# Seven part products for a third group of four expert tiles in a Fourier and expert layer on one core

## The chip, the core and the metric

The kernel runs on one core of one Trainium2 chip. Its engines work side by side: PE (TensorE) multiplies 128 x 128 weight tiles with columns that stream past them, and PEld is PE's loading of those weights; DVE (VectorE) and ACT (ScalarE) do element-wise work and can read the accumulators (PSUM banks); POOL (GpSimd) does element-wise work on SBUF only; SP (SyncE) issues nearly all DMAs from one queue, in order. Each engine runs its own instruction list in order, so an instruction that waits holds up everything behind it on that engine.

The metric is the device time of one execution in microseconds (us); less is better. The profile is one further execution, recorded instruction by instruction.

## The reference

The layer takes 2048 tokens of width 512, normalizes them, and adds three things: the input, a two-dimensional Fourier transform of the normalized input (given as matrices; real part), and an expert layer that picks 2 of 4096 experts per token and head.

```python
xn = _layernorm(x)
return x + _A_ref(xn, ...) + _B_ref(xn, ...)

# A: y = Cr @ (xn Wr^T) - Ci @ (xn Wi^T)
# B, with 32 heads, dk = 128, 64 x 64 = 4096 experts:
q = einsum("nd,dhc->nhc", xf, w_q)
s1 = einsum("nhd,ed->nhe", q[..., :dk], k1)
s2 = einsum("nhd,ed->nhe", q[..., dk:], k2)
# two best of s1 and of s2, their 4 sums, the 2 best of those -> top_e, top_s
g = softmax(top_s)
act = gelu(einsum("nd,nhkd->nhk", xf, u[top_e]))
out = einsum("nhk,nhk,nhkd->nd", g, act, v[top_e])
```

## The kernel before

**Precision.** Float32 operands are split into a float16 high part and a float16 low part, and a product is three matmuls (high-high, high-low, low-high) into a float32 bank.

**Stages.** (1) Up to about 77 us: layer norm and the Fourier part. (2) The score stage, to 420 us: for each of 8 chunks of 4 heads (`j`) and 16 token tiles of 128 (`i`), PE computes the scores (`s_mm`, line 252), ACT moves them out of the bank (line 951), DVE finds the largest ones (lines 955, 959), and `routing` on POOL, DVE and ACT turns the indices of a chunk into experts and weights. In the same 128 steps, at step numbers set by hand in the list `todo`, ACT and POOL prepare everything that the later stages read: they scale and split `w_q` (`m_prep`, lines 162 to 167), the expert inputs `u` and outputs `v` (`fill_uv`, lines 780 to 782), and store in DRAM the sums of `u` blocks (`sum_u`) and of token blocks (`sum_x`). (3) The expert stage, to the end: rather than gather, the kernel multiplies every token with all 4096 experts (`z` phases, 16 groups of 256 experts), makes a one-hot weight matrix from the routing (`g_mm`, PE line 1252, fed by DVE lines 1242 to 1250), multiplies it with the activations (`w_part`) and multiplies the outcome with all of `v` (`v` phases, line 1297).

**A pair phase.** Six of the `z` phases handle two token tiles at once (tiles 2 and 3, 4 and 5, to 12 and 13); between two of them stand two `v` phases. A group of 256 experts is multiplied in one of two ways:

- *plain tile*, `u_part` (line 1095, "c" in the order string): 24 matmuls of 256 columns, one bank, then two GELUs on ACT (line 1102) that empty the bank;
- *part products*, `slot` (line 1164): four groups together (a "quad") are seen as a 2 x 2 by 2 x 2 block product, which takes 7 block products in place of 8 when some of them are made from sums of blocks. Each part product is 24 matmuls of 128 columns. The part products 1, 6, 7, 4 add up in one bank (X), 5 and 3 in another (Z), 2 has a third (Y), and between them ACT copies intermediate values out (lines 1198, 1203, 1205, 1211), DVE adds (1200, 1208, 1212) and ACT applies the GELU (1191). PE may add to X again only when ACT has copied the value before.

Before the change groups 8 to 15 form two quads, groups 0 to 7 are plain. The order of a pair phase is a string, quads a and b:

```python
SEQ = "1a 5a 2a c 6a c 3a c 7a c 1b 5b 4a 2b c 6b c 3b 7b c c 4b".split()
```

Four banks (`banks`) go round in the order in which they were given back, so PE can also wait for the bank that it takes next. Part products 5, 6, 7 and 3 read a sum of `u` blocks (512 KB), which is loaded from DRAM into a ring of three buffers. `ring_plan` decides beforehand, from nominal durations, which buffer each load takes and after which part product it is issued; `ring_load` issues it on SP.

**Checks along the way.** The kernel checks that the given matrices are the Fourier matrices and that nothing overflows; a slower general path follows if not. For that, "units" load pieces of the inputs during the expert stage: `compare` loads a tile `cx` (lines 1326, 1327), DVE subtracts what it should be (1328 to 1353), ACT sums what is left (1373); `fit` loads `w_q` (1424) for ACT to sum. A pair phase has three `compare` units and one `fit`.

The order of the instructions on each engine is set by a scheduler that keeps the dependencies of the program and moves instructions within them.

Of the kernel before, what the change touches and what calls it, by code (L numbers as in the profile page):

```python
# [20 lines left out]
D = 512  # L21
# [7 lines left out]
XS = 512.0  # L29
V1 = 5  # L30
V2 = 9
QUADS = (8, 10, 12, 14), (9, 11, 13, 15)
PAIRS = tuple(range(2, 14, 2))


# [1 line left out]
def tile_fnet_peer(ctx, tc, x, ca, cb, c5, wt, wf, wr, wq, kt, ut, vn, out):  # L37
# [117 lines left out]
    def m_prep(j, t, pool, at):  # L155

        raw = MS[j, t].rearrange("p h k -> p (h k)")
        MS[j, t, "h"] = pool.tile([P, 2, D], F16, tag="wh", name=f"wh{j}_{t}", bufs=4)
        h = MS[j, t, "h"].rearrange("p h k -> p (h k)")
        l = raw.bitcast(F16)[:, 0:2 * D]  # L160
        MS[j, t, "l"] = l.rearrange("p (h k) -> p h k", h=2)
        nc.scalar.activation(h, raw, AF.Copy, scale=at)
        if t > (1 if j == 2 else 0):
            nc.scalar.activation(raw, raw, AF.Copy, scale=at)
        else:
            nc.gpsimd.tensor_scalar(raw, raw, sw, None, op0=ALU.mult)
        nc.gpsimd.tensor_tensor(l, raw, h, op=ALU.subtract)
# [553 lines left out]
    def part_b(safe, stS, stP, stQ, stE, xt, u_sb, cmp_p, w4):  # L721
# [65 lines left out]
        def scratch(g):  # L787
            return v_sb[g].rearrange("p l c d -> p (l c d)").bitcast(F32)
# [11 lines left out]
        def sum_u(g, part, at=None):  # L800

            qd, t = next((n, q.index(g)) for n, q in enumerate(QUADS) if g in q)
            s4 = scratch(8 - t % 2)
            if part == 0:
                raw = SRAW.pop(g)
                a = [raw[:, c, k * 256:k * 256 + 256] for c in range(2) for k in range(2)]
                r = [s4[:, k * 256:k * 256 + 256] for k in range(4)]
                nc.gpsimd.tensor_tensor(r[0], a[2], a[3], op=ALU.add)
# [4 lines left out]
            split4(part - 1, s4, v_sb[6].rearrange("p l c d -> p (l c d)")[:, t % 2 * 2 * D:t % 2 * 2 * D + 2 * D],  # L813
                   lambda i: s_d[qd].rearrange("o p (t l f) -> t l p o f", t=4, l=2)[t, i], at)

        def sum_x(b, part, at=None):

            n = (0, 2, 4, 5, 7, 5)[PAIRS.index(b)]
            f, t4 = scratch(n), scratch(n + 1)
            if part == 0:  # L820
                v = xq[b // 2]
                nc.gpsimd.tensor_copy(f[:, 0:1], behind(one, at))
                nc.gpsimd.tensor_tensor(f.rearrange("p (q f) -> p q f", q=2),  # L823
                                        v[:, :, 0].rearrange("p q k n -> p q (k n)"),
                                        v[:, :, 1].rearrange("p q k n -> p q (k n)"), op=ALU.add)
                b11, b21, b12, b22 = [f[:, k * 256:k * 256 + 256] for k in range(4)]
# [149 lines left out]
        else:  # L976
# [12 lines left out]
        fills = [divmod(n, 16) for n in (0, 1, 2, 8, 3, 10, 16, 4, 12, 14, 17, 5, 9, 11, 18, 6, 13, 15, 19, 7, 20,  # L989
                                         21, 22, 23, 24)]  # L990
        slots = [29, 31, 36, 43, 45] + [16 * j + i for j in range(3, 7) for i in (4, 6, 11, 13)]
        slots += [119 + 2 * n for n in range(len(fills) - len(slots))]
        assert fills[slots.index(119)] == (1, V1)
        for (which, g), n in zip(fills, slots):
            todo[n].append(lambda at, w=which, g=g: fill_uv(w, g, at))
            todo[n - (3 if n < 119 else 1)].append(lambda at, w=which, g=g: fill_load(w, g))
            if which == 0 and not safe and any(g in q for q in QUADS):
                todo[n + 5].append(lambda at, g=g: (sum_u(g, 1, at), sum_u(g, 2)))
        if not safe:
            for n, b in zip((19, 22, 25, 107, 111, 114), PAIRS):  # L1000
                todo[n].append(lambda at, b=b: sum_x(b, 0, at))
                todo[n + (4 if n == 114 else 5)].append(lambda at, b=b: (sum_x(b, 1, at), sum_x(b, 2)))
# [101 lines left out]
        if not safe:  # L1104
            sx = stE.enter_context(tc.tile_pool(name="sx", bufs=1, side="left"))
            x4 = sx.tile([P, 2, 4, 2, P], F16, name="x4")
            PLAIN = [g for g in range(16) if not any(g in q for q in QUADS)]
            SEQ = "1a 5a 2a c 6a c 3a c 7a c 1b 5b 4a 2b c 6b c 3b 7b c c 4b".split()
            OPS = {"1": (0, None, None, 0), "2": (1, None, None, 1), "5": (None, 0, 0, None), "6": (None, 1, 1, None),
                   "3": (None, 3, None, 3), "7": (None, 2, 2, None), "4": (3, None, 3, None)}  # L1110

        USES = []
        if not safe:
            clock = 0
            for n in range(len(PAIRS)):
                for o in SEQ:
                    ns = 2616 if o == "c" else 1344
                    if o != "c" and OPS[o[0]][1] is not None:
                        USES.append((clock, clock + ns, ("ab".index(o[1]) + n) % 2, OPS[o[0]][1]))
                    clock += ns  # L1120
                clock += 50000
        RING = {}
# [48 lines left out]
        def z_pair(b, n, after):  # L1171

            cgs = iter(PLAIN)
            st = {}
            total, done, cg = sum(2616 if o == "c" else 1344 for o in SEQ), 0, 0
            for o in SEQ:
                if o == "c":
                    u_part(b, next(cgs))
                    done += 2616
                else:  # L1180
                    op, qd = o[0], ("ab".index(o[1]) + n) % 2
                    quad = QUADS[qd]

                    def dst(a, c):
                        return ACT[b[c]][:, 2 * quad[0] + a:2 * quad[3] + 2:2 * (quad[1] - quad[0]), :]

                    def v(p):
                        return p.rearrange("p (t n) -> p t n", t=4)

                    def gelu(d, src=None):  # L1190
                        nc.scalar.activation(d, d if src is None else src, AF.Gelu_apprx_tanh, scale=zsc)  # L1191

                    if op in "125":
                        st[o[1], "X" if op == "1" else "Y" if op == "2" else "Z"] = take(f"z{op}_{b[0]}_{qd}")
                    (X, Xt), (Y, Yt), (Z, Zt) = [st.get((o[1], k), (None, None)) for k in "XYZ"]
                    slot(op, quad, Z if op in "53" else Y if op == "2" else X, qd)
                    if op == "1":
                        nc.scalar.activation(dst(0, 0), v(X), AF.Copy)
                    elif op == "2":
                        nc.vector.tensor_tensor(dst(0, 0), v(Y), dst(0, 0), op=ALU.add)  # L1200
                        banks.append(Yt)
                    elif op == "5":
                        nc.scalar.activation(dst(1, 0), v(Z), AF.Copy)
# [565 lines left out]
```

## Time and profile before

| What | Value |
|---|---|
| Median of 3 runs | 1145.59 us (1145.26 to 1149.68) |
| The profiled execution's own time | 1145.57 us |
| Its span, first to last instruction | 1143.8 us |
| Busy in the span: PE, DVE, ACT, POOL | 98%, 83%, 56%, 27% |
| DMA, mean over the span | 173 GB/s |
| Score stage | about 77 to 420 us |
| Six pair phases | 490.6 to 531.9, 577.4 to 621.4, 666.8 to 710.8, 756.2 to 798.8, 844.3 to 888.4, 933.8 to 977.4 us |

A row of a timeline or of a group reads: engine, line, operation, out<-in, shapes, number of instructions, duration, and the idle time of the engine just before with the instruction that ended it ("<-"). In a timeline a merged row's duration runs to the end of its last matmul, which overlaps the next one's start; the distance from one start to the next is what it costs. PEclk is the share of the full TensorE clock that was granted.

### The profile page before, as it was taken

The numbers are of one execution on the slowest core, as the hardware profiler recorded it, in microseconds if no ns is written. First come the engines' busy times: TensorE is split into PE (matmuls) and PEld (weight loads), VectorE is DVE, ScalarE is ACT, GpSimd is POOL, SyncE is SP. The second block draws the span as 40 slices with busy tenths as digits, with TensorE's granted clock in tenths as the row PEclk, the third lists the DMA queues.
The fourth block names the chain that finished last, engine by engine and source line by source line (L and its number), as shares of the span: only waits on it lengthen the run. The fifth ranks groups of instructions, "written<-read, shape, count | busy, mean of one in ns | idle before, by whom it ended". The sixth has DMA issues, their size and how long they took to land.

```text
span 1143.8 us, 27323 instructions
## 1 busy us (share of the span) xinstructions
PE 1123.1 (98%) x10748; PEld 726.1 (63%) x10748; DVE 949.7 (83%) x2855; ACT 642.1 (56%) x1086; POOL 312.3 (27%) x342
## 2 busy tenths in 40 slices
PE   9999999999999999999999999999999999999997
PEld 6455454544544469687487488479478569567763
DVE  7899979989889899956985895895996886889782
ACT  6557598788787374454444445435435534545542
POOL 1415896887888730000000000000010010000000
PEclk8999999999999999999999999999999999999999
DMA  9884455435333216453752762763663654565743
GB/s 283 278 208 162 164 167 188 140 110 194 114 134 105 75 51 207 157 210 123 259 180 101 243 222 92 229 213 119 222 206 131 219 198 145 186 235 174 237 148 105
DMA packets 114856, 198.36 MB, mean 173 GB/s; under 512 B 34068, under 2 KB 57499, under 8 KB 114718
## 3 DMA queue, kind: packets, MB, share of 16 engines
q1 hardware_dynamic: 114416, 196.45, 51.5%
q8 instruction: 86, 1.41, 0.5%
q14 instruction: 52, 0.43, 0.1%
q10 hardware_dynamic: 302, 0.08, 0.1%
HBM read 165.75 MB, written 24.97 MB: 167 GB/s over the span
## 4 chain that ended last, share of the span: by engine, by line
PE 50%; DVE 7%; DMA 5%; POOL 2%; ACT 2%; issue 1%; SPq 0%; ACTq 0%; POOLq 0%; DVEq 0%
PE v L1297 24%; PE z L1095 14%; PE z L1164 7%; DMA cx<-in_cb_dram 4%; PE g L1252 4%; PE s L252 2%; DVE L L1242 1%; DVE w L1260 1%; DVE cx L1347 1%; DVE act L1268 1%; ACT cx L1373 1%; POOL v L823 1%; DMA fit<-in_wq_dram 1%; DVE R L1247 0%; DVE R L1250 0%
## 5 line engine op out<-in xcount | busy, mean ns | idle before, releaser
L252 PE MATMUL s<-m,xq 128*128 128x512 f16 x1344 | 297.4, 379 | 2.5 <-ACT ss L951 2.5
L1297 PE MATMUL v<-v,act 128*128 128x512 f16 x1056 | 233.3, 379 | 0.0
L252 PEld LDWEIGHTS <-xq 128*128 128x128 f16 x1344 | 129.7, 98 | 153.5 <-issue 3.8
L1095 PE MATMUL z<-xb,u 128*128 128x128 f16 (+1 forms) x2688 | 219.9, 242 | 5.0 <-ACT act L1191 4.7
L1095 PEld LDWEIGHTS <-u 128*128 128x128 f16 x2688 | 196.7, 98 | 18.2 <-issue 5.6
L1310 POOL TENSOR_TENSOR y<-y,xr 128x512 f32<-128x512 f32 x15 | 24.6, 1643 | 638.8 <-DMA y<-y_d 380.5
L1242 DVE TENSOR_TENSOR L<-io_lam,cmp 128x2048 f16<-128x2048 f16 x128 | 158.4, 1237 | 41.3 <-PE g L1252 41.3
L1297 PEld LDWEIGHTS <-act 128*128 128x128 f16 x1056 | 101.2, 98 | 117.6 <-issue 0.2
L955 DVE MAX8 vals<-ss 128x8 f32<-128x64 f32 x896 | 133.4, 216 | 3.0 <-ACT ss L951 3.0
L951 ACT ACTIVATE ss<-s,wsc 128x512 f32<-128x512 f32 x120 | 81.7, 684 | 44.1 <-PE s L252 35.5
L1297 PE MATMUL v<-v,w 128*128 128x512 f16 x480 | 106.2, 379 | 0.0
L1373 ACT ACTIVATE cx<-cx 128x896 f32<-128x896 f32 x64 | 60.4, 943 | 63.5 <-DVE cx L1353 49.0
L959 DVE FIND_INDEX8 idx<-vals,ss 128x8 uint16<-128x256 f32 x224 | 93.8, 419 | 0.0
L1267 ACT ACTIVATE act<-w 128x1024 f16<-128x1024 f32 x36 | 48.4, 1360 | 69.2 <-DVE w L1260 69.0
L1297 PEld LDWEIGHTS <-w 128*128 128x128 f16 x480 | 45.9, 98 | 53.4
L1102 ACT ACTIVATE act<-z,scl 128x256 f32<-128x256 f32 (+1 forms) x88 | 44.1, 525 | 49.5 <-PE z L1095 49.5
L1252 PEld LDWEIGHTS <-L 128*128 128x128 f16 x2048 | 60.2, 96 | 12.0 <-issue 1.5
L1260 DVE SCALAR_TENSOR_TENSOR w<-act,scl,g 128x1024 f32<-128x1024 f32 x44 | 55.7, 1276 | 13.4 <-ACT act L1191 13.4
L1347 DVE TENSOR_TENSOR cx<-cx 128x512 f32<-128x512 f32 (+2 forms) x84 | 48.4, 610 | 18.6 <-DMA cx<-in_cb_dram 18.5
L1164 PEld LDWEIGHTS <-s 128*128 128x128 f16 x1080 | 62.7, 98 | 0.5
L1252 PE MATMUL g<-R,L 128*128 128x32 f16 x2048 | 62.0, 176 | 1.0 <-DVE R L1250 0.9
L1268 DVE TENSOR_TENSOR act<-w,act 128x1024 f16<-128x1024 f32 x44 | 59.2, 1348 | 2.3 <-ACT act L1267 2.3
(363 smaller groups left out, 1729.2 us busy)
## 6 DMA issues: line engine op xcount, KB each, us to landing
v<-v_d SPq DMA_DIRECT2D x67, 512.0 KB, 4.6
cx<-in_cb_dram SPq DMA_DIRECT2D x64, 448.0 KB, 5.4
s<-s_d SPq DMA_DIRECT2D x35, 512.0 KB, 4.5
w<-in_wq_dram SPq DMA_DIRECT2D x28, 512.0 KB, 6.1
fit<-in_wq_dram SPq DMA_DIRECT2D x28, 512.0 KB, 4.3
uv<-in_vn_dram SPq DMA_DIRECT2D x16, 512.0 KB, 4.0
uv<-in_ut_dram SPq DMA_DIRECT2D x16, 512.0 KB, 4.0
c<-in_ca_dram SPq DMA_DIRECT2D x8, 512.0 KB, 7.5
```

What stands on the lines that cost most here:

```text
L252: nc.tensor.matmul(ps, xt[i][:, l, kd, :], m[:, r, kd, :], start=(n == 0), stop=(n == 3 * KD - 1))
L951: nc.scalar.activation(s, ps, AF.Copy, scale=inv)
L955: nc.vector.max(vals[:, i, w, :, h], s[:, g, :])
L959: nc.vector.max_index(idx[:, i, w].rearrange("p k h -> p (k h)"), vals[:, i, w, 0:2].rearrange("p k h -> p (k h)"), s[:, w * HC:g + 1, :]. ...
L1095: nc.tensor.matmul(ps if n == 1 else ps.rearrange("p (b n) -> p b n", b=2), ug[:, l, c % 2, kd, :], xb2[:, k0, r, kd, :] if n == 1 else xb ...
L1164: nc.tensor.matmul(bank[:, t * P:(t + 1) * P], lt, rt, start=(t == k == 0 and op in "125"), stop=(t == 3 and k == 5), skip_group_check=op ...
L1242: nc.vector.tensor_tensor(L.rearrange("p t (l two) -> p t l two", two=2), io_lam.rearrange("p (l two) -> p l two", two=2).unsqueeze(1).to_ ...
L1252: nc.tensor.matmul(p[:, hf, t * NC:(t + 1) * NC], L[:, t, :], R[:, t, :], start=True, stop=True)
L1260: nc.vector.scalar_tensor_tensor(w, act[:, :, ts], fw, p.rearrange("p h (n c) -> p c (h n)", c=NC), op0=ALU.mult, op1=ALU.mult)
L1268: nc.vector.tensor_tensor(w16[..., 1], w, w16[..., 0], op=ALU.subtract)
L1297: nc.tensor.matmul(pv, w16[:, c, :, l], v_sb[g][:, r, cc, :], start=(n + cc == 0 and k == 0), stop=(n == 15 and cc == 1 and k == 2))
L1373: later.append(lambda: nc.scalar.activation(tf[:, P:], tf[:, P:], AF.Abs, accum_out=chk[:, n:n + 1]))
```

## The change

Groups 4 to 7 become a third quad, so that only groups 0 to 3 stay plain in the pair phases; the two single-tile phases at each end keep 16 plain groups. A pair phase then has 21 part products and 4 plain tiles in place of 14 and 8, in a new order with single plain tiles between part products; in every other pair phase the quads' order is reversed (`turn_q`). The ring loads 10 sums in the second to sixth pair phase, 6 before.

In the score stage groups 4 to 7 get their sums (`sum_u`: four additions or subtractions on POOL, a copy on ACT, a subtraction on POOL, two stores of 256 KB each); ACT in place of POOL scales the first quarter of `w_q` for `j` = 3 to 7; the order of the fills and three of the steps of `sum_x` change, and with them its scratch tiles.

```diff
-QUADS = (8, 10, 12, 14), (9, 11, 13, 15)
+QUADS = (8, 10, 12, 14), (9, 11, 13, 15), (4, 5, 6, 7)
...
         nc.scalar.activation(h, raw, AF.Copy, scale=at)
-        if t > (1 if j == 2 else 0):
+        if t > 1 or j > 2:
             nc.scalar.activation(raw, raw, AF.Copy, scale=at)
         else:
             nc.gpsimd.tensor_scalar(raw, raw, sw, None, op0=ALU.mult)
...
-            s4 = scratch(8 - t % 2)
+            par = [f for w, f in fills if w == 0 and any(f in q for q in QUADS)].index(g) % 2
+            s4 = scratch(8 - par)
...
-            n = (0, 2, 4, 5, 7, 5)[PAIRS.index(b)]
+            n = (0, 2, 4, 4, 7, 5)[PAIRS.index(b)]
...
-        slots += [119 + 2 * n for n in range(len(fills) - len(slots))]
+        slots = slots[:-1] + [113] + [119 + 2 * n for n in range(4)]
...
-            for n, b in zip((19, 22, 25, 107, 111, 114), PAIRS):
+            for n, b in zip((19, 22, 25, 106, 109, 118), PAIRS):
...
-            SEQ = "1a 5a 2a c 6a c 3a c 7a c 1b 5b 4a 2b c 6b c 3b 7b c c 4b".split()
+            SEQ = "1a 5a 2a 6a c 3a 1b 7a 2b 5b 4a 6b c 3b 1c 7b 2c 5c 4b 6c c 3c 7c c 4c".split()
+
+            def turn_q(k, n):
+                return ("abc" if n % 2 else "cba").index(k)
...
-                    op, qd = o[0], ("ab".index(o[1]) + n) % 2
+                    op, qd = o[0], turn_q(o[1], n)
```

What this does to the engines' lists shows at three places. In them `cx9` to `cx11` are the tiles of three `compare` units, `z1_4_q`, `z2_4_q` and `z5_4_q` the banks X, Y and Z of quad `q` for tiles 4 and 5, `z4_n` the bank of the n-th plain tile, and `sq_k_n` a ring buffer with sum k of quad q, loaded after the n-th use of the ring. Line numbers in the changed kernel are up to 4 higher.

ACT in the second pair phase (tiles 4 and 5), before:

```order
L1373 ACTIVATE cx10_8897,sums_87<-cx10_8897 128x896
L1102 ACTIVATE act4_8248<-z4_3_8537,scl_93 128x256
L1102 ACTIVATE w4_126<-z4_3_8537,scl_93 128x256
L1373 ACTIVATE cx11_8984,sums_87<-cx11_8984 128x896
L1198 ACTIVATE act4_8248<-z1_4_0_8568 128x4x128
L1203 ACTIVATE act4_8248<-z5_4_0_8594 128x4x128
L1191 ACTIVATE act4_8248<-z1_4_1_8249,scl_93 128x4x128
```

ACT at the same place, now:

```order
L1377 ACTIVATE cx10_9070,sums_87<-cx10_9070 128x896
L1195 ACTIVATE w4_126<-w4_126,scl_93 128x4x128
L1202 ACTIVATE act4_8366<-z1_4_2_8793 128x4x128
L1377 ACTIVATE cx11_9184,sums_87<-cx11_9184 128x896
L1215 ACTIVATE w4_126<-z1_4_1_8572 128x4x128
L1195 ACTIVATE w4_126<-w4_126,scl_93 128x4x128
L1195 ACTIVATE act4_8366<-act4_8366,scl_93 128x4x128
L1207 ACTIVATE act4_8366<-z5_4_2_8923 128x4x128
L1195 ACTIVATE act4_8366<-z1_4_1_8572,scl_93 128x4x128
```

Behind the sum over `cx11` there stood two copies of the second quad and the GELU that empties bank X of the first; now the first instruction behind it is the copy of part product 7 of the second quad, which its part product 4 waits for.

SP in the same phase, before:

```order
L1424 DMA fit7_8649<-in_wq_dram 128x1024
L1326 DMA cx9_8744<-in_ca_dram 128x128
L1327 DMA cx9_8744<-in_cb_dram 128x896
L1326 DMA cx10_8897<-in_ca_dram 128x128
L1147 DMA s0_0_10_8478<-s_d_61 128x2048
L1327 DMA cx10_8897<-in_cb_dram 128x896
L1326 DMA cx11_8984<-in_ca_dram 128x128
L1327 DMA cx11_8984<-in_cb_dram 128x896
L1147 DMA s0_1_11_8532<-s_d_61 128x2048
```

SP at the same place, now:

```order
L1428 DMA fit7_8820<-in_wq_dram 128x1024
L1151 DMA s1_1_14_8569<-s_d_61 128x2048
L1330 DMA cx9_8917<-in_ca_dram 128x128
L1331 DMA cx9_8917<-in_cb_dram 128x896
L1151 DMA s1_3_15_8622<-s_d_61 128x2048
L1330 DMA cx10_9070<-in_ca_dram 128x128
L1151 DMA s1_2_16_8678<-s_d_61 128x2048
L1331 DMA cx10_9070<-in_cb_dram 128x896
L1330 DMA cx11_9184<-in_ca_dram 128x128
L1151 DMA s2_0_17_8731<-s_d_61 128x2048
L1331 DMA cx11_9184<-in_cb_dram 128x896
```

One ring load stood between the loads of the three `compare` tiles; now a ring load stands ahead of each of them, and each of those waits for PE to end a part product.

POOL early in the last chunk of the score stage (`g6` is the routing weight of chunk 6, `v6`, `v8` scratch tiles), before:

```order
L795 TENSOR_TENSOR v6_921<-v6_921,v5_920 128x1024
L924 CAST z_826<-lc6_0_5210 128x16x2x4 x2
L924 CAST z_826<-di6_0_5202 128x16x2x4 x2
L822 COPY v5_920<-ss7_2_5185 128x1
L823 TENSOR_TENSOR v5_920<-xq6_109 128x1024
L828 TENSOR_TENSOR v6_921<-v5_920 128x256
L830 TENSOR_TENSOR v6_921<-v5_920 128x256
L829 TENSOR_TENSOR v6_921<-v5_920,v6_921 128x256
L831 TENSOR_TENSOR v6_921<-v5_920,v6_921 128x256
L895 TENSOR_TENSOR g6_0_5274<-c106_0_5163,g6_0_5274 128x16x4
L795 TENSOR_TENSOR v8_923<-v8_923,v7_922 128x1024
```

POOL at the same place, now:

```order
L782 TENSOR_TENSOR v4_919<-uv1_4_5108,v4_919 128x1024
L925 CAST z_826<-lc6_0_5246 128x16x2x4 x2
L896 TENSOR_TENSOR g6_0_5308<-c106_0_5195,g6_0_5308 128x16x4
L795 TENSOR_TENSOR v8_923<-v8_923,v7_922 128x1024
L925 CAST z_826<-di6_0_5238 128x16x2x4 x2
L823 COPY v5_920<-ss7_6_5364 128x1
L824 TENSOR_TENSOR v5_920<-xq6_109 128x1024
```

The sums of the last token pair (five instructions from `xq6` on) stood ahead of the routing weight; now they stand behind it, and a fill's subtraction stands ahead.

More of the change, by code (lines that the diff above doesn't have):

```diff
@@ L812, in sum_u @@
                 return
-            split4(part - 1, s4, v_sb[6].rearrange("p l c d -> p (l c d)")[:, t % 2 * 2 * D:t % 2 * 2 * D + 2 * D],
+            split4(part - 1, s4, v_sb[6].rearrange("p l c d -> p (l c d)")[:, par * 2 * D:par * 2 * D + 2 * D],
                    lambda i: s_d[qd].rearrange("o p (t l f) -> t l p o f", t=4, l=2)[t, i], at)
         def sum_x(b, part, at=None):
-            n = (0, 2, 4, 5, 7, 5)[PAIRS.index(b)]
+            n = (0, 2, 4, 4, 7, 5)[PAIRS.index(b)]
             f, t4 = scratch(n), scratch(n + 1)
@@ L988, in part_b @@
                         lambda at, j=j, t=t: m_prep(j, t, wqp, behind(sw, at)))
-        fills = [divmod(n, 16) for n in (0, 1, 2, 8, 3, 10, 16, 4, 12, 14, 17, 5, 9, 11, 18, 6, 13, 15, 19, 7, 20,
-                                         21, 22, 23, 24)]
+        fills = [divmod(n, 16) for n in (0, 1, 2, 8, 3, 10, 4, 16, 12, 14, 5, 17, 9, 11, 6, 18, 13, 15, 7, 19, 20,
+                                         23, 24, 21, 22)]
         slots = [29, 31, 36, 43, 45] + [16 * j + i for j in range(3, 7) for i in (4, 6, 11, 13)]
-        slots += [119 + 2 * n for n in range(len(fills) - len(slots))]
-        assert fills[slots.index(119)] == (1, V1)
+        slots = slots[:-1] + [113] + [119 + 2 * n for n in range(4)]
         for (which, g), n in zip(fills, slots):
@@ L999, in part_b @@
         if not safe:
-            for n, b in zip((19, 22, 25, 107, 111, 114), PAIRS):
+            for n, b in zip((19, 22, 25, 106, 109, 118), PAIRS):
                 todo[n].append(lambda at, b=b: sum_x(b, 0, at))
-                todo[n + (4 if n == 114 else 5)].append(lambda at, b=b: (sum_x(b, 1, at), sum_x(b, 2)))
+                todo[n + (4 if n == 118 else 5)].append(lambda at, b=b: (sum_x(b, 1, at), sum_x(b, 2)))
         for g, n in zip(range(V2, 16), (25, 38, 41, 57, 73, 89, 105)):
@@ L1118, in part_b @@
                     if o != "c" and OPS[o[0]][1] is not None:
-                        USES.append((clock, clock + ns, ("ab".index(o[1]) + n) % 2, OPS[o[0]][1]))
+                        USES.append((clock, clock + ns, turn_q(o[1], n), OPS[o[0]][1]))
                     clock += ns
```

## Prediction

> **What bounds the kernel now.** I began with the busy times of the page.
>
> ```profile
> PE 1123.1 (98%) x10748; PEld 726.1 (63%) x10748; DVE 949.7 (83%) x2855; ACT 642.1 (56%) x1086; POOL 312.3 (27%) x342
> ```
>
> PE is busy for 1123.1 of 1143.8 us, so what the change does to PE's own work counts in full, and what it does elsewhere counts only where PE comes to wait. An average over stages can hide such waits; next I looked at the table of windows. Its columns are the window, its length, busy time (and instructions) of PE, PEld, DVE, ACT and POOL, the granted clock, the DMA share and GB/s. The first six rows are the pair phases, called P0 to P5 here; then come a burst inside P2 and 45 us of the score stage.
>
> ```profile
> 490.60:531.90 41.30, 41.30 (x593) 39.12 (x592) 21.16 (x49) 19.52 (x39) 1.52 (x1) 1.00 0.35 125
> 577.40:621.40 44.00, 42.55 (x631) 40.09 (x628) 29.44 (x46) 20.20 (x40) 1.48 (x1) 1.00 0.42 143
> 666.80:710.80 44.00, 42.49 (x631) 40.06 (x628) 29.58 (x47) 20.26 (x40) 2.48 (x1) 1.00 0.42 143
> 756.20:798.80 42.60, 42.28 (x631) 39.98 (x628) 29.69 (x48) 20.54 (x40) 1.74 (x1) 1.00 0.42 147
> 844.30:888.40 44.10, 42.35 (x633) 40.06 (x630) 33.08 (x62) 20.30 (x40) 1.75 (x1) 1.00 0.41 142
> 933.80:977.40 43.60, 42.51 (x632) 40.09 (x629) 29.72 (x49) 20.39 (x40) 2.35 (x1) 1.00 0.39 132
> 675.00:687.00 12.00, 12.00 (x165) 11.18 (x162) 9.06 (x15) 5.42 (x12) 0.00 (x0) 1.00 0.94 321
> 305.00:350.00 45.00, 45.00 (x293) 21.96 (x292) 41.14 (x213) 36.37 (x54) 37.10 (x37) 1.00 0.38 133
> ```
>
> Length less PE's busy time is PE's idle time: 0, 1.45, 1.51, 0.32, 1.75 and 1.09 us in P0 to P5, together 6.1 us. In the score stage PE loses nothing in these 45 us. The table of waits names what ended PE's idle times: the first four rows for the pair phases, the last for the score stage.
>
> ```profile
> PE z L1095 <- ACT act L1191: 4.7, 4, 1.8
> PE z L1164 <- ACT act L1102: 0.5, 1, 0.5
> PE z L1164 <- ACT w L1102: 0.5, 1, 0.5
> PE z L1095 <- ACT w L1191: 0.3, 1, 0.3
> PE s L252 <- ACT ss L951: 2.5, 1, 2.5
> ```
>
> So PE waits in the pair phases for GELUs on ACT that empty a bank, 4.7 of 6.0 us for L1191. Why ACT is late shows in the chain through P1 (start, duration, what).
>
> ```profile
> 581.56 2.62 PE z L1095 x24
> 584.18 1.34 PE z L1164 x24
> 585.52 0.79 PE g L1252 x32
> ...
> 590.31 0.33 SPq L1147
> ...
> 590.69 6.61 DMA cx<-in_cb_dram
> ...
> 597.32 0.96 DVE cx L1347
> ...
> 601.19 1.03 ACT cx L1373 x2
> 602.22 0.49 ACT act L1198
> 602.71 0.49 ACT act L1203
> 603.20 0.59 ACT act L1191
> ...
> 603.83 2.78 PE z L1095 x24
> ```
>
> A ring load waits on SP for PE to end a part product (590.31). The load of a `compare` tile stands behind it and takes 6.61 us; its sum on ACT ends only at 602.22, and two copies and the GELU that PE needs stand behind that.
>
> **The change part by part.**
>
> *PE's work.* A plain tile costs PE 2.62 us and a part product 1.34 us (the first two rows of that chain). Seven part products in place of four plain tiles: 7 x 1.34 = 9.38 for 4 x 2.62 = 10.48 us, 1.10 less in each of six phases, **-6.6 us**. PE stands back to back here, so this lies on the path.
>
> *The wait in P1 to P5.* Before, the bank that the late GELU empties is wanted 1.34 us after its last part product (one part product, 2b, stands between). In the new order 6b, a plain tile and 3b stand between 4a and the next use: 1.34 + 2.62 + 1.34 = 5.3 us, more than the whole wait. So the known stall goes. What is late next: `cx11` now waits on SP behind the ring load that PE's 6b releases, and behind its sum stands the copy that 4b needs (both orders above). With the new order's durations (three `g_mm` at 0.79 among them) 6b ends 18.2 us into the phase; then 0.33 + 0.05 issue, 6.61 + 0.02, 0.96, 1.03 and 0.49 make 27.7, while 4b is due at 28.3: 0.6 us of slack, and 1c and 5b, by the same kind of sum, stand little better. From one side the stalls could all vanish (0), from the other stay at the mean that P1 to P5 show (6.1 / 5 = 1.2) or exceed it (rival C). Since the old cause is gone and the new slack is about as small as the durations vary, I take 0.7 each, 3.5 in all.
>
> *P0* has no idle time now. Its bounds change, though:
>
> ```profile
> 501.43 0.95 ACT L1373 ACTIVATE cx<-cx 128x896 f32<-128x896 f32 x1 [1.24 <-issue]
> ```
>
> The GELUs of the first plain tile come to stand behind this sum, which ends at 502.5; two of them make it 503.3, and 2b, which takes that bank, is due 12.0 us after 490.6, at 502.6. I take 1.0 us, between 0 and 2.9 (0.7 plus a tile that lands 2.2 late, rival C). All pair phases: 1.0 + 3.5 = 4.5 in place of 6.1, **-1.6 us**.
>
> *DMA.* Four more loads of 512 KB per phase: 143 GB/s x 44.0 us is 6.3 MB, plus 2.1 MB, over about 41 us is 204 GB/s. The burst above moved 321 GB/s at a share of 0.94, so there is room on average, not within a burst. The landings now (first row: number, size, median; then min/median/max; then one of three loads that were issued together):
>
> ```profile
> s<-s_d SPq DMA_DIRECT2D x35, 512.0 KB, 4.5
> DMA to landing us min/median/max: 3.2/4.5/5.9
> s_-1_6778<-s_d SPq DMA_DIRECT2D x1, 512.0 KB, 8.8
> ```
>
> The planner's rule with the new order gives leads (from the end of the part product that releases a buffer to the use) of 8.0 us for six loads of a phase and 6.7 for three; they were 7.9 to 22. The slowest ring load of the phases needs 5.9, so I cost them at nothing. SP is held at each until PE releases it; `fit`, `xr` and `cx` loads stand behind, and of these only `cx` ends in something that PE waits for (above).
>
> *Score stage.* POOL and ACT get other work (us busy, mean ns, idle before):
>
> ```profile
> L166 POOL TENSOR_SCALAR w<-w,wsc 128x1024 f32<-128x1024 f32 x7 | 19.9, 2845 | 24.6 <-ACT wh L162 24.6
> L795 POOL TENSOR_TENSOR v<-v,v 128x1024 f16<-128x1024 f32 x14 | 29.9, 2134 | 21.8 <-ACT v L794 21.8
> L808 POOL TENSOR_TENSOR v<-uv 128x256 f32<-128x256 f32 x8 | 6.1, 763 | 0.0
> L164 ACT ACTIVATE w<-w,ss 128x1024 f32<-128x1024 f32 x17 | 19.6, 1154 | 0.2
> L794 ACT ACTIVATE v<-v,ss 128x1024 f16<-128x1024 f32 x14 | 16.1, 1147 | 0.2
> ```
>
> POOL: five scalings less (-14.2), four subtractions of L795 (+8.5) and 16 small ones of L808's size (+12.2): +6.5. ACT: 5 x 1.154 + 4 x 1.147 = +10.4. Both had 8 of 45 us free in the window above, and a stage of 343 us holds nearly eight such windows; PE's 45.00 of 45.00 covers it, and without that cover up to 10.4 us of it would show. The eight stores of 256 KB fall where the DMA share is 0.38: nothing. What does reach PE is the one loss of 2.5 us, and its beginning is in these rows of POOL and DVE:
>
> ```profile
> 393.21 0.32 POOL L895 TENSOR_TENSOR g<-c,g 128x64 f32<-128x64 f32 x1
> 393.49 2.13 POOL L795 TENSOR_TENSOR v<-v,v 128x1024 f16<-128x1024 f32 x1
> 393.57 2.13 DVE L896 CAST z<-g 128x128 f16<-128x128 f32 x1 [2.38 <-POOL g L895]
> ...
> 401.56 4.69 PE L252 MATMUL s<-m,xq 128*128 128x512 f16 x21 [2.46 <-ACT ss L951]
> ```
>
> DVE waited 2.38 us for the routing weight, which stood on POOL behind the sums of a token pair, and then its cast took 2.13. Now the weight stands ahead of these five, but behind a fill's 2.13; the cast can meet the same L795. I take half of the loss as gone, **-1.2 us**, between -2.5 (all) and +2.5 (POOL's longer backlog doubles it).
>
> The cast's rows elsewhere:
>
> ```profile
> L896 DVE CAST z<-g x9: 171/1278/2131, 125.0 to 434.6; 128x128 f16<-128x128 f32 x7, 128x32 f16<-128x32 f32 x1, 128x96 f16<-128x96 f32 x1
> ```
>
> Its longest run lies exactly beside POOL's subtraction. The Trainium skill, page "SBUF — State Buffer", section "Who interferes with whom", says that a DVE cast in a two-port mode and POOL exclude each other for a whole instruction; the trace agrees, with 2.13 us for both. By that rule POOL's added work slows DVE even where POOL has time to spare, which is rival F.
>
> *Sum:* -6.6 - 1.6 - 1.2 = -9.4 us on the profiled execution's 1145.57 (span 1143.8 and 1.8 around it), which is the median's 1145.59 as well: **1136 us**.
>
> **Rivals.**
>
> *B, all waits go.* No new wait in the phases and none in the score stage: -6.6 - 6.1 - 2.5 = -15.2, 1130.4 us. For it: 5.3 us of room at the old place. Against: slacks of half a microsecond at new ones.
>
> *C, `compare` tiles land late.* Four more loads share the burst. If `cx11` takes 8.8 us, as the third of three loads issued together did, in place of 6.61, 4b waits 2.2 - 0.6 = 1.6 more: 2.3 each in P1 to P5, 1.5 in P0, 13.0 in place of 6.1, and nothing gained in the score stage: 1145.57 - 6.6 + 6.9 = 1145.9. Against: the loads of a phase are spaced by part products, not issued together.
>
> *D, slower: ring loads land late.* With 8.8 and 0.2 for the issue, six loads are 1.0 late and three 2.3, 12.9 us per phase; each wait also gives time to the two loads in flight, so about a third counts: 4.3 x 6 = 25.8, and with the other terms 1145.57 - 9.4 + 25.8 = 1162. It decides once a landing exceeds 6.7 us. Against: 5.9 is the longest of these landings, at 42% DMA share.
>
> *E, slower: weight loads bind.*
>
> ```profile
> L1164 PEld LDWEIGHTS <-s x1080: 95/98/98, 505.1 to 969.8; 128*128 128x128 f16 x180
> ```
>
> A part product loads 24 weights at up to 98 ns, 2.35 us. If these no longer overlapped one another, seven would take 16.5 in place of 10.48, +6.0 x 6 = +36, about 1179. Against: 24 take 1.34 us in the chain, 55.8 ns each, in the same code. The Trainium skill, page "TensorE: Matmul & The Clock Gate", section "Back-to-back issue gap", gives some 81 ns for a 128-column matmul with its weight load in a sustained stream; by that a part product takes 1.94 us, and an estimate of the whole is about 1162. The rows measure 55.8, and I go by them.
>
> *F, POOL's work hits DVE in the score stage.* Three more losses like the 2.46 at 401.56, 7.4 us, with no gain there: 1145.57 - 6.6 - 1.6 + 7.4 = 1144.8. Against: DVE was free to stall nowhere else in the stage, at the POOL load of 37.10 in 45.
>
> **How the numbers follow.** Forecast 0.46, with a range of its own of 1132 to 1141 (stalls of the phases 0.3 to 1.7 each, score stage -2.5 to +1); B 0.17, C 0.17, F 0.08, D 0.10, E 0.02. The 0.5% that a measurement can tell is 5.7 us, 1139.9 to 1151.3. Nearly all of the forecast and B are faster, 0.62; C, F and the forecast's upper edge are the same, 0.26; D and E are slower, 0.12. Leaving out D, E and the outer edges, the range is 1129.5 to 1149.
>
> **What would show it.** Right: pair phases of 41 to 42 us, in which PE's rows at L1164's place stay 1.34 us apart; no wait for L1191's GELU of quad a; ring landings below 6.5 us; a score stage that ends no later than now. Wrong: PE waits released by a DMA of `s` (D), ACT's sum over `cx` just ahead of a copy that PE waits for in every phase (C), part products further apart than 1.34 us (E), or new waits of L252 with a cast beside POOL behind them (F).

## The result, and the profile after

The changed kernel takes 1133.0 us (median of 6 runs, 1131.42 to 1134.83) against 1146.02 us for the kernel before in the same comparison: a ratio of 0.9883, 95% interval 0.9866 to 0.9901, so 11.3 to 15.4 us less. The profiled executions have spans of 1143.8 and 1130.4 us, 13.4 apart.

The busy times of the page after the change:

```profile
PE 1114.2 (99%) x11180; PEld 724.4 (64%) x11180; DVE 960.3 (85%) x2873; ACT 657.5 (58%) x1099; POOL 319.4 (28%) x357
```

PE is busy 8.9 us less and still bounds the kernel; DVE, ACT and POOL have more to do than before. The table of windows for the six pair phases, with the columns as in the prediction, shows where the time went:

```profile
488.70:529.50 40.80, 40.45 (x666) 39.20 (x665) 22.71 (x51) 20.55 (x39) 1.71 (x1) 1.00 0.50 178
574.90:615.90 41.00, 41.00 (x702) 39.92 (x699) 31.61 (x49) 21.94 (x40) 2.41 (x1) 1.00 0.56 203
661.30:702.80 41.50, 41.31 (x706) 40.10 (x703) 32.04 (x50) 21.94 (x40) 1.32 (x1) 1.00 0.57 202
748.10:789.20 41.10, 41.10 (x706) 40.03 (x703) 31.64 (x51) 22.12 (x40) 2.26 (x1) 1.00 0.58 204
836.00:877.80 41.80, 41.35 (x705) 40.10 (x702) 35.03 (x65) 21.61 (x40) 2.04 (x1) 1.00 0.57 200
923.10:964.20 41.10, 41.10 (x706) 40.03 (x703) 31.64 (x52) 21.94 (x40) 2.36 (x1) 1.00 0.54 191
```

P1, P3 and P5 have no PE idle time left; P0, P2 and P4 have 0.35, 0.19 and 0.45 us, at the GELUs of a plain tile (2b waits), at 4a and at 4b. The load on DMA rose from about 143 to 200 GB/s, as worked out. What ended PE's waits after the change, from the score stage on:

```profile
PE g L1256 <- DVE R L1254: 1.5, 3, 1.0
PE v L1301 <- DMA v<-v_d: 1.0, 1, 1.0
PE s L252 <- ACT ss L952: 0.5, 1, 0.5
PE z L1168 <- ACT w L1215: 0.4, 1, 0.4
PE z L1168 <- ACT act L1102: 0.3, 1, 0.3
PE z L1168 <- ACT act L1215: 0.2, 1, 0.2
```

The 4.7 us for L1191 are gone. What is left there is small: copies (L1215) and the GELUs of P0's first plain tile (L1102). Two waits between the pair phases, for DVE at 835.6 and for a load of `v` at 1007.4, one us each, are new.

Adding up by stages, from the starts of PE's rows in the two timelines (a pair phase runs to the end of its last part product, the stretches between hold the `v` phases):

| Stretch | Before | After | Difference |
|---|---|---|---|
| Score stage | 342.42 | 340.62 | -1.80 |
| Six pair phases | 259.32 | 246.88 | -12.44 |
| Six stretches behind them | 272.85 | 275.22 | +2.37 |
| Last stretch, to the end of the span | 121.02 | 119.58 | -1.44 |
| All else (start, first single-tile phases) | 148.19 | 148.10 | -0.09 |

### The profile page after: what moved, and what is told of

It is laid out like the page before. It is cut to its first block, busy times and chain, and to the rows that moved or that the text cites. A ratio compares the mean times of both kernels' runs of the same rounds, so it can differ in the third digit from the quotient of the medians.

```text
span 1130.4 us, 28284 instructions
## 1 busy us (share of the span) xinstructions
PE 1114.2 (99%) x11180; PEld 724.4 (64%) x11180; DVE 960.3 (85%) x2873; ACT 657.5 (58%) x1099; POOL 319.4 (28%) x357
## 4 chain that ended last, share of the span: by engine, by line
PE 50%; DVE 10%; DMA 3%; ACT 2%; POOL 2%; issue 1%; SPq 0%; DVEq 0%; ACTq 0%; POOLq 0%
PE v L1301 24%; PE z L1168 13%; PE z L1095 10%; PE g L1256 4%; DMA cx<-in_cb_dram 3%; DVE L L1246 2%; DVE vals L956 1%; DVE idx L960 1%; DVE w L1264 1%; DVE act L1272 1%; DVE cx L1351 1%; DVE R L1251 0%; DMA fit<-in_wq_dram 0%; DVE cx L1340 0%; POOL v L824 0%
## 5 line engine op out<-in xcount | busy, mean ns | idle before, releaser
L252 PE MATMUL s<-m,xq 128*128 128x512 f16 x1344 | 297.4, 379 | 1.0 <-ACT ss L952 0.5
L252 PEld LDWEIGHTS <-xq 128*128 128x128 f16 x1344 | 129.8, 98 | 152.2 <-issue 2.4
L1095 PE MATMUL z<-xb,u 128*128 128x128 f16 (+1 forms) x2112 | 154.3, 234 | 0.1
L1095 PEld LDWEIGHTS <-u 128*128 128x128 f16 x2112 | 141.4, 98 | 6.6 <-issue 0.2
L1168 PEld LDWEIGHTS <-s 128*128 128x128 f16 x1656 | 94.8, 98 | 0.1
L1168 PE MATMUL z<-x,s 128*128 128x128 f16 x1248 | 78.1, 219 | 0.0
L1168 PEld LDWEIGHTS <-u 128*128 128x128 f16 x1296 | 74.9, 98 | 1.8 <-issue 1.4
L1256 PEld LDWEIGHTS <-L 128*128 128x128 f16 x2048 | 60.3, 96 | 12.7 <-issue 2.1
L1264 DVE SCALAR_TENSOR_TENSOR w<-act,scl,g 128x1024 f32<-128x1024 f32 x44 | 55.8, 1277 | 10.3 <-ACT act L1195 10.3
```

The source lines that it names most:

```text
L252: nc.tensor.matmul(ps, xt[i][:, l, kd, :], m[:, r, kd, :], start=(n == 0), stop=(n == 3 * KD - 1))
L1095: nc.tensor.matmul(ps if n == 1 else ps.rearrange("p (b n) -> p b n", b=2), ug[:, l, c % 2, kd, :], xb2[:, k0, r, kd, :] if n == 1 else xb ...
L1168: nc.tensor.matmul(bank[:, t * P:(t + 1) * P], lt, rt, start=(t == k == 0 and op in "125"), stop=(t == 3 and k == 5), skip_group_check=op ...
L1256: nc.tensor.matmul(p[:, hf, t * NC:(t + 1) * NC], L[:, t, :], R[:, t, :], start=True, stop=True)
L1264: nc.vector.scalar_tensor_tensor(w, act[:, :, ts], fw, p.rearrange("p h (n c) -> p c (h n)", c=NC), op0=ALU.mult, op1=ALU.mult)
```

## The experiments

Each experiment was timed beside the kernel before on the same chip; ratios have 95% intervals. "P sum" is the length of the six pair phases in the profiled execution, 259.32 us before. A pair phase of two quads that waits for nothing is 42.12 us long (41.32 for P0), 251.92 in all; with three quads it is 41.02 (40.22), 245.32 in all. These are the shortest phases in the executions below; undisturbed ones repeat to 0.02 us. What a phase is longer than that is taken as its waits; it comes out somewhat larger than the idle time that the views list (1.56 us for 0.99 in the changed kernel).

### The order alone (two_room)

```diff
-SEQ = "1a 5a 2a c 6a c 3a c 7a c 1b 5b 4a 2b c 6b c 3b 7b c c 4b".split()
+SEQ = "1a 5a 2a c 6a c 3a c 7a c 1b 5b 4a 2b 6b c c 3b 7b c c 4b".split()
```

> The kernel before with one swap in the order of a pair phase: the plain tile that follows part product 2b now follows 6b, so that the bank of quad a which its last GELU empties is asked for 2.68 us after the end of 4a, not 1.34. Theory 1 (the waits come from asking for that bank too early): the longest such wait was 1.75 us, so 1.34 us more room leaves at most 0.4 of it, the 5.0 us of waits for L1191 all but go, the 1.0 us of waits for L1102 stay; about 1141.1. Theory 2 (ACT is late by itself, because of the sums over the compare tiles, and the wait only moves to the next bank): 3 us or more of waits stay, 1143.5 to 1145.5.

Measured: 1140.76 us, ratio 0.9948 (0.9927 to 0.9968), some 5.6 us less. P sum 252.43. Its waits from the score stage on:

```profile
PE s L252 <- ACT ss L951: 2.4, 1, 2.4
PE g L1252 <- DVE R L1250: 1.8, 4, 0.9
PE v L1297 <- DMA v<-v_d: 0.3, 1, 0.3
```

No wait of L1095 or L1164 is left, not even those for L1102 that were expected to stay. One swap, without a third quad, ends nearly all of the old waits (P sum is 0.5 us over the undisturbed 251.92): theory 1 holds, and in this execution the wait does not move to the next bank. With the same swap a later execution (two_room_score, below) has 2.24 us of waits left, most of them in P4.

### The compare tiles (before_no_cx, before_skip_cx, after_skip_cx)

Two kernels without the 18 `compare` units of the pair phases; the first lets the later units move up, the second leaves all others at their places.

```diff
-                    for cg in (9, 12, 15) if len(ph) == 3 else (0, 2, 3, 6):
+                    for cg in () if len(ph) == 3 else (0, 2, 3, 6):
```

> The kernel before without the compare units of the six pair phases (18 of 68 units; that part of the check of the given matrices is left out). Both theories of the old waits hold that a sum over a compare tile stands ahead of the GELU: the 6.0 us of waits in the pair phases go, about 1139.6. Rival (ACT is late through the part products' own copies and GELUs): at least 3 us of waits for L1191 stay, 1142.5 or more.

Measured: 1145.19 us, ratio 0.9989 (0.9974 to 1.0004). By the time alone the rival would have won. The waits say otherwise:

```profile
PE g L1252 <- DVE R L1250: 7.5, 7, 2.8
PE s L252 <- ACT ss L951: 2.4, 1, 2.4
```

All waits for L1191 are gone, P sum is 251.91, and 7.5 us of waits for DVE (0.9 before) have come in outside the pair phases: the edit changed DVE's work in other phases. So it was made again:

```diff
-                        put(ph, cg, U)
+                        put(ph, cg, SKIP if len(ph) == 3 else U)
```

> A cleaner form of before_no_cx: the 18 compare units that stand in the pair phases are skipped there (that part of the check is left out; two one-column memsets on POOL take the place of each), and all other units stay at their places, where before_no_cx had moved them up and so put DVE work elsewhere. Theory 1 (the 6.0 us of waits in the pair phases came from the compare tiles, and before_no_cx gave as much back in new waits for DVE, 7.5 us, that its moved units made): 6 us under the kernel before, 1139.5 to 1141. Theory 2 (something else in the pair phases takes the place of these waits): 1143.5 or more.

Measured: 1135.88 us, ratio 0.9912 (0.9876 to 0.9948). P sum is 251.91 again, 7.4 us less than before, and the waits for DVE are 0.5 us:

```profile
PE s L252 <- ACT ss L951: 2.5, 1, 2.5
...
PE g L1252 <- DVE R L1250: 0.5, 2, 0.3
```

Theory 1 holds: either without the tiles or with more room for the bank the old waits all but vanish; both the late ACT and the early demand were needed. The gain of 10 us is more than the 6 expected. Of it, 7.4 us are the pair phases (the view of waits lists only 6.0 of them), 1.5 us the last stretch, and the rest of the profiled difference of 10.6 us is the first stage, which none of the edits touches; it took 75.6 to 79.0 us in the profiled executions of all these kernels, at a granted clock of 0.93 to 1.00 in it. The kernel before also scatters more: 1141.57 to 1149.9 us over 14 runs beside this one's 1135.06 to 1137.2 over 5.

The same edit in the changed kernel:

> The same edit in the changed kernel. Theory 1 (what is left of waits in its pair phases, 1.0 to 1.8 us, are ACT copies behind sums over compare tiles): these go, 1 to 2 us under the changed kernel, 1131 to 1132.5. Theory 2 (the third quad's loads, not the compare tiles, make them): unchanged, 1133 or more.

Measured: 1130.31 us, ratio to the kernel before 0.9855 (0.9812 to 0.9898). The time fell, but not for theory 1's reason: P sum is 247.12, no less than the 246.88 with the tiles. Of the 2.5 us between the profiled executions 1.7 are in the stretches behind the pair phases, where the wait for a load of `v` is missing (it is missing in after_wq_pool too, with the tiles in place), and 1.3 in the first and the last stage; 0.4 went the other way. In the pair phases two waits for L1215 are left, of 0.67 and 0.81 us, and the chain to the first shows why:

```profile
582.77 5.25 DMA fit<-in_wq_dram
...
588.39 1.15 ACT fit L1429 x2
589.55 0.49 ACT w L1215
...
590.08 2.00 PE z L1168 x33
```

It is the `fit` unit: its load of 512 KB stands behind a ring load on SP, its sum on ACT ahead of the copy that 4a waits for. The second, in P4, is of the same kind. So both theories fall in part: the waits behind a compare tile, in P0 and at 4b in P4 (below), are gone, and longer ones at 4a behind `fit` have come in; with the tiles there was one of these, of 0.19 us in P2.

### The score stage alone (before_new_score)

```diff
-        if t > (1 if j == 2 else 0):
+        if t > 1 or j > 2:
...
-            for n, b in zip((19, 22, 25, 107, 111, 114), PAIRS):
+            for n, b in zip((19, 22, 25, 106, 109, 118), PAIRS):
```

(and the new places of the last five fills, with the scratch tiles that go with them)

> The kernel before with the changed kernel's score stage alone, as far as it can be had without a third quad: ACT scales the first quarter of w_q from j = 3 on, the last fills and the sums of three token pairs stand at the new steps. Two quads, old order. Theory 1 (the one loss of the stage came from the sums of the last token pair ahead of the routing weight on POOL): the 2.46 us go to 0.5 or less, about 1143.5. Theory 2 (that loss depends on what else the change does in the stage): it stays, 1145.5.

Measured: 1142.6 us, ratio 0.9962 (0.9941 to 0.9983). The score stage takes 339.69 us, 2.73 less, and the wait of L252 for L951 is not in the list any more. Theory 1 holds. In the same execution the pair phases waited more than before, P sum 263.8:

```profile
PE z L1094 <- ACT act L1190: 4.8, 4, 2.4
PE z L1163 <- ACT w L1101: 2.0, 1, 2.0
```

Nothing in the pair phases was edited here, and the engines' lists there are the same; the old order's waits differ that much from one execution to another (7.4 us and 11.9 us over the undisturbed length).

How the changed kernel avoids the loss shows in its POOL and DVE rows:

```profile
389.15 0.32 POOL L896 TENSOR_TENSOR g<-c,g 128x64 f32<-128x64 f32 x1
389.43 2.13 POOL L795 TENSOR_TENSOR v<-v,v 128x1024 f16<-128x1024 f32 x1
```

```profile
391.97 0.20 DVE L897 CAST z<-g 128x128 f16<-128x128 f32 x1
```

The weight is ready at 389.5, ahead of the five instructions for the last token pair, which start at 398.4. DVE still has other work then and does not wait for it, and the cast comes after L795 has ended: 0.20 us in place of 2.13. It took 0.20 us as well in before_new_score, two_room_score, after_again and after_wq_pool, where the weight also stands ahead.

### w_q back on POOL (after_wq_pool)

```diff
-        if t > 1 or j > 2:
+        if t > (1 if j == 2 else 0):
```

> The changed kernel with one edit undone: POOL in place of ACT scales the first quarter of w_q for j = 3 to 7 again, five instructions of 2.85 us. Theory 1 (POOL has about 5 us of 45 to spare in the stage, and this takes 1.9): no more than 1 us slower, 1132.5 to 1134. Theory 2 (POOL was full with the sums of the third quad, and its lateness reaches PE through DVE's routing): three or more losses of about 2.5 us in the score stage, 1140 or more.

Measured: 1132.11 us, ratio to the kernel before 0.9871 (0.9841 to 0.9901). Its score stage is 341.80 us, 1.2 longer, and L252 waits 1.4 us in place of 0.5; in the time nothing of it can be told. By the trace this part of the change is worth about 1 us.

### Order and score stage together, and the third quad's own part (two_room_score, after_again)

The swap of the first experiment and the score stage of the kernel above, still two quads:

> The kernel before with two of the changes that already showed something, together: the swap of two_room and the score stage of before_new_score. Still two quads and eight plain tiles. Theory 1 (the waits in the pair phases and the loss of the score stage are separate and add): about 5.5 + 2.5 = 8 us under the kernel before, 1138. Theory 2 (one is only the other, seen twice): no better than two_room, 1140.5 or more. What is left to the changed kernel is then the third quad's own part: by part products alone 6.6 us.

> The changed kernel itself, beside two_room_score on one chip. Theory 1 (the third quad is worth what PE saves, 6 x 1.10 = 6.6 us, less the 1.0 us of waits in its pair phases and 2.0 us of new waits for DVE and a v load): 3.5 to 6.6 us under two_room_score. Theory 2 (the third quad's other costs, DMA and DVE work, eat what PE saves): within 2 us of two_room_score.

Measured: 1137.89 us (ratio 0.9915, 0.9888 to 0.9941) and 1133.81 us (0.9889, 0.986 to 0.9919). The two gains add, 8.6 us of 12.7 without any third quad. The third quad brings 4.1 more by the medians. The two intervals overlap, and though each of the four runs (1131.76 to 1134.74 us) is below each of the five with two quads (1134.83 to 1140.64), the times alone settle this last step only barely. The traces settle it for the pair phases: P sum is 254.16 and 247.82, of which 2.24 and 2.50 us are waits, and the rest differs by the 6.60 us that seven part products save against four plain tiles.

### Plain tiles in clumps (after_clump)

```diff
-SEQ = "1a 5a 2a 6a c 3a 1b 7a 2b 5b 4a 6b c 3b 1c 7b 2c 5c 4b 6c c 3c 7c c 4c".split()
+SEQ = "1a 5a 2a 6a 3a 1b 7a 2b 5b 4a 6b 3b 1c 7b 2c 5c 4b 6c 3c c 7c c c 4c c".split()
```

> The changed kernel with the plain tiles not spread: the order of a pair phase is 1a 5a 2a 6a 3a 1b 7a 2b 5b 4a 6b 3b 1c 7b 2c 5c 4b 6c 3c c 7c c c 4c c. PE's work is the same; the leads of six ring loads fall from 8.0 to 5.4 us, and 4a and the next use of its bank stand 2.7 us apart, not 5.3. Theory 1 (the plain tiles cover the ring loads and the emptying of banks): landings of 4.8 us in the middle and 5.9 at the longest, with the issue, are late by up to 1 us for some of the six, and ACT's copies behind compare tiles by up to 1 us: 1 to 2 us per phase, 1139 to 1145. Theory 2 (their place does not matter as long as the part products take less PE time): within 1.5 us of the changed kernel.

Measured: 1144.37 us, ratio to the kernel before 0.9973 (0.9954 to 0.9993). The same part products in another order lose nearly all of the gain, about 11 us:

```profile
PE z L1168 <- DMA s<-s_d: 5.6, 7, 1.3
PE z L1168 <- ACT act L1207: 2.7, 3, 1.2
...
PE z L1168 <- DVE act L1204: 1.9, 1, 1.9
...
PE z L1168 <- ACT w L1207: 0.8, 1, 0.8
```

Ring loads are late by up to 1.3 us where the lead is 5.4, and ACT and DVE come late to values that part products wait for. Theory 1 holds.

### A ring of two buffers (after_ring2)

```diff
-                    free = [p for p in range(3) if p not in held]
+                    free = [p for p in range(2) if p not in held]
```

> The changed kernel with a ring of two buffers in place of three: leads of 4.0 us for five loads of a phase and 5.3 for five (now 6.7 to 8.0), 72 loads in all in place of 62. Theory 1 (a ring load becomes the bound where issue and landing, 0.4 + 4.8 us, pass the lead): five loads a phase are about 1.2 us late, less a third that the next one gains back, 4 us per phase, about 1157, range 1148 to 1165, with waits of L1168 that a DMA of s ends. Theory 2 (DMA has so much room that landings shorten when loads are spread less): under 1140.

Measured: 1142.11 us, ratio to the kernel before 0.9974 (0.9954 to 0.9995). Neither number fits: 8 to 9 us slower than the changed kernel, where 24 were expected by theory 1 and less than 7 by theory 2. The kind of wait is theory 1's:

```profile
PE z L1168 <- DMA s<-s_d: 8.8, 10, 1.9
```

Ten waits, where I had counted five late loads in each of six phases: a late load also moves every later use, so one wait pays for more of the loads behind it than the third that I took off. That is an argument that no run tried.

### A fourth quad (four_quads, four_quads_ring4)

```diff
-QUADS = (8, 10, 12, 14), (9, 11, 13, 15), (4, 5, 6, 7)
+QUADS = (8, 10, 12, 14), (9, 11, 13, 15), (4, 5, 6, 7), (0, 1, 2, 3)
```

> The changed kernel with a fourth quad (0, 1, 2, 3): 28 part products and no plain tile in a pair phase, 1a 5a 2a 6a 3a 1b 7a 2b 5b 4a 6b 3b 1c 7b 2c 5c 4b 6c 3c 1d 7c 2d 5d 6d 3d 7d 4c 4d. PE's work falls by another 6.6 us; most leads are 5.4 us, as in after_clump, and POOL gets 4 x (2.13 + 2.97) = 20.4 us more in the score stage. Theory 1 (spreading is worth more than the fourth quad): after_clump's waits of 11 us against 6.6 gained, 1134 to 1142. Theory 2 (PE's work decides): under 1131.

> four_quads with a fourth ring buffer, its 4 KB taken from the pool of work tiles (three in place of four, which w_part, compare and fit share). Leads are 8.06 us for most loads. Theory 1 (without late ring loads only ACT's and DVE's waits of after_clump, 4 to 6 us, stand against 6.6 gained): 1129 to 1134. Theory 2 (three work tiles hold up DVE's and ACT's units and g_mm's products): over 1136.

Measured: 1150.05 us (ratio to the kernel before 1.003, 1.0007 to 1.0053) and 1160.74 us (1.0111, 1.0065 to 1.0156), slower than both kernels. With three buffers:

```profile
PE z L1168 <- DMA s<-s_d: 8.8, 10, 1.7
PE z L1168 <- ACT act L1207: 5.0, 6, 1.4
PE m L148 <- POOL w L167: 3.6, 1, 3.6
```

With four buffers and three work tiles:

```profile
PE g L1256 <- DVE R L1254: 10.2, 7, 4.2
PE z L1168 <- ACT act L1207: 9.0, 6, 2.2
PE m L148 <- POOL w L167: 3.6, 1, 3.6
```

The fourth buffer ends the waits for ring loads, and P sum falls from 258.97 to 254.30, but more is lost elsewhere: 8.6 of the 10.2 us of waits for DVE lie behind the last pair phase, where the ring is not used, and in the chains there a load into a work tile starts only when ACT has ended its sum over another. This points at the missing work tile; the two halves of the edit were not run apart. In both kernels POOL is late in the score stage, which got only the sums of groups 0 to 3 as new work; it is 346.1 us long in the first, 5.5 more. Theory 1 of the first and theory 2 of the second hold in kind, but 1150 lies well over the 1134 to 1142 that were given. With three buffers and no plain tile left, ring loads and ACT's copies are both waited for in every pair phase, and POOL's lateness had not been counted.

## Why the prediction was right, and where its sizes were off

The forecast was 1136 us, 9.4 less; 13.4 were gained in the profiled execution and 13.0 by the medians. The signs of all three terms were right, and so were their main causes. That the time fell inside the forecast's own range of 1132 to 1141 is in part luck: the waits of the pair phases came out below the least that was allowed (0.3 us each), and only 0.8 us of net loss at places that had not been forecast brought the profiled execution from some 1131.3 up to 1132.17. The range's upper edge does not follow from its parts either: 1.7 us in each phase and +1 in the score stage would give 1144, not 1141.

**PE's work, -6.6: right.** The undisturbed phases differ by 251.92 - 245.32 = 6.60 us. Part products stayed 1.34 us apart, so rival E is out.

**Waits in the pair phases, -1.6: the mechanism right, the size too small.** P sum shows 7.4 us of waits before and 1.56 after, -5.84; by PE's idle time, the measure of the forecast, it is 6.1 and 0.99, -5.1. The first half of the step, that the known stall goes since the bank is asked for 5.3 us after its last part product, is borne out by the swap experiment, where 2.68 us were enough. The second half, 4.5 us of new waits, was mis-sized. The place was right. In P4 the chain to the wait at 4b is the one that I worked out for P1:

```profile
851.70 0.33 SPq L1151
...
852.08 6.09 DMA cx<-in_cb_dram
...
863.43 1.04 ACT cx L1377 x2
864.47 0.49 ACT w L1215
...
865.01 2.00 PE z L1168 x33
```

PE was idle 0.45 us there, and the phase is 0.70 us longer than an undisturbed one. In P1 no wait came, though the ring load (593.25) and the use (603.17) stand where I had them, 18.4 and 28.3 us into the phase:

```profile
593.25 0.33 SPq L1151 DMA_DIRECT2D s<-s_d  x1
593.62 0.43 SPq L1331 DMA_DIRECT2D cx<-in_cb_dram  x1
```

```profile
600.30 0.95 ACT L1377 ACTIVATE cx<-cx 128x896 f32<-128x896 f32 x1 [0.28 <-DVE cx L1357]
601.16 0.19 ACT L1377 ACTIVATION_READ_ACCUMULATOR cx<-cx 128x1 f32 x1
601.25 0.58 ACT L1215 ACTIVATE w<-z 128x512 f32<-128x512 f32 x1
```

The copy ended at 601.8, leaving 1.3 us of slack, not 0.6: from the issue to the sum's start it took 6.68 us, against 7.59 in my layout. That layout took the 6.61 us landing of the old chain, a load in a burst: the DMA share was 1.00 in those 6.6 us, at 342 GB/s, and 0.88, at 317, behind the new issue. The 0.7 us that I then charged to each phase, about half of the old mean, had no row behind it. In P0 the wait stood where it was worked out and was 0.35 us, not 1.0. And one place I had not seen: the copy that 4a waits for stands behind a `fit` sum, which the experiment without compare tiles brought out; the wait in P2 is of this kind. Which of these places shows a wait varies: in after_again, the same kernel, 4b in P1 did wait 0.86 us, behind a compare tile's load of 7.65 us, and 4a waited behind `fit` in P3 and P4, 0.68 and 0.23 us.

**Ring loads, 0: right.** Their landings after the change (min/median/max):

```profile
DMA to landing us min/median/max: 3.1/4.8/5.9
```

The longest is still 5.9, under the shortest lead of 6.7. The view knows the landing of only 7 of these 59 loads, as it knew 5 of 35 before, so this alone would prove little; what shows that rival D did not happen is that no wait of PE in the table above was ended by a load of `s`. The two-buffer ring and the clumps show that such waits do come once the leads are shorter. Rival C fell as a whole, since the compare tiles' loads land no later, rather sooner; those of them that the view knows (one in eight or nine), before:

```profile
DMA to landing us min/median/max: 3.0/5.0/7.1
```

and after:

```profile
DMA to landing us min/median/max: 2.6/4.4/6.4
```

The packets in the trace tell more: taken in order, 128 of 3584 bytes to a load, they have the last tile of P1 to P5 arrive 5.4 to 6.7 us after its issue before and 4.5 to 5.8 us after. The 7.65 us in after_again show that one can still come a microsecond later than in the forecast's layout; it then cost one phase 0.86 us. (The rival's own sum took 1.5 us for P0, where the forecast's bound for that case was 2.9.)

**Score stage, -1.2: right mechanism, -1.8 measured.** Of the 2.46 us 0.5 remain; the cast met nothing. Rival F's price, put to the test by giving POOL 14 us more, was 1.2 us.

**What was left out:** +2.4 us between the pair phases. I had costed the loads and the DVE work of the units at nothing there. The two new waits are:

```profile
835.63 0.55 PE L1256 MATMUL g<-R,L 128*128 128x32 f16 x16 [1.01 <-DVE R L1254]
1007.43 2.75 PE L1301 MATMUL v<-v,act 128*128 128x512 f16 x12 [1.00 <-DMA v<-v_d]
```

They are 2.0 of the 2.4 us here; in the second profile of the same kernel the stretches are only 1.3 us longer than before (275.22 and 274.16 in place of 272.85). The chain to the first runs through DVE back to a compare tile's load of 5.94 us; what makes the `v` load late stays open. Against this, the last stretch is 1.4 us shorter, also not forecast: 0.9 of it is the last write's landing, 6.63 us before and 5.69 after. It was 5.3 to 5.8 us in the seven other executions with three or four quads and in before_no_cx and before_skip_cx, and 6.5 to 6.7 in two_room, two_room_score and before_new_score; why stays open.

## What to carry to other kernels

Where an engine waits for a buffer, ask both how late it comes free and how soon it is wanted: here one swap of two entries in a table was worth 5.6 us of the 13, without any new computation. A part of the work that runs long and needs little (the plain tile) is cover; spread one at a time it hid loads and copies that, with the same work clumped, cost 11 us, and with none of it left cost more than the fourth quad saved. A view of landings, or one profiled execution, is a sample: ask how many loads it knows, and whether the waits stand at the same place the next time. When an ablation shows no gain, look whether the waits went or were only replaced: taking the compare tiles out gave 1 us in its first form and 10 in its second, with the same pair phases in both.

## What the runs showed of the hardware that was not expected

The same DVE cast of 128x128 took 2.13 us beside a POOL subtraction of 2.13 us that started 0.08 us earlier, and 0.20 us where that subtraction had ended; the slow one ended 0.08 us after the subtraction. The Trainium skill, page "SBUF — State Buffer", section "Who interferes with whom", has the two engines exclude each other for a whole instruction when such a cast runs in a two-port mode; the two rows agree with it.

PE's 128-column matmuls ran 55.8 ns apart (24 in 1.34 us) in phases of 14 and of 21 part products, with the weight load of each; the 81 ns that the page "TensorE: Matmul & The Clock Gate" of the Trainium skill, section "Back-to-back issue gap", gives for a sustained stream was not seen.
